# Layer 2's input product by seven half-size products for two of three pairs of chunks, and layer 2 in the order of the list scheduler

## Chip, cores and metric

One core of one Trainium2 chip. The metric is the device time of one execution in microseconds (us), the median of the runs. Engines: TensorE (PE; its weight loads PEld), VectorE (DVE), ScalarE (ACT), GpSimd (POOL), SyncE (SP, which issues most DMAs).

## What is computed

Attention with a threshold (4 batches, 8 heads, 576 positions, head size 64), then a gated layer with an RMS norm ("layer 1"), then a layer with a cosine ("layer 2"). The attention output is laid out as 2304 tokens by 512.

```python
# layer 1: x is 2304 x 512, w_gate and w_val 512 x 1536, w_out 1536 x 512
xn = x / sqrt(mean(x * x) + 1e-6) * rms_g
x = (silu(xn @ w_gate) * (xn @ w_val)) @ w_out
# layer 2: w_in 512 x 2048, w_out 2048 x 512
h = x @ w_in
out = (h * cos(h)) @ w_out
```

## The kernel before

**Matmuls.** Each operand of a product in the two layers is held as a rounded high part and a low rest (`hi`, `lo`, float32r), and `mm3` (L803 to L805) makes three matmuls of each 128-row step: high by high, high by rest, rest by high. All matmuls of both layers have line L805. A pair of weights arrives as 64-bit numbers; converting one 128x512 tile (`conv` in `moe`, L1032; `weight_job` for layer 2, L343) takes two bit operations on VectorE, a scaling on ScalarE and a sum on GpSimd; splitting it takes a copy on ScalarE and a subtraction on VectorE.

**Tokens** are worked on in 6 chunks of 384 (`TC`), as pairs (0,1), (2,3), (4,5).

**Attention and layer 1** are put in order by a list scheduler, `Plan`. Every step is added with its kind, a time at which it is due and what it needs, takes and frees (buffers counted by tag, as `c` for 4 PSUM banks of products, `h` for 6 hidden tiles, `w` for 6 weight tiles). `STEPS` gives each kind an engine, a duration in ns and an offset of its place in the order. `order()` simulates the engines and takes, again and again, the step that can start first, ties by place. Kinds in `LOCK` share one simulated port between VectorE and GpSimd; a GpSimd step in `BEHIND` also gets a wait for the last VectorE step that held the port.

**Layer 1's input products** (`block`, in `moe`) are made by seven products (`PROD`) where the plain form has eight: a block is a pair of chunks, and the gate and value tiles of one 128-column tile of the hidden layer. The seven use the weight combinations G, A22, S24, S31 and the token combinations B11, B21, B22, T1 to T4; VectorE adds the seven results up in SBUF tiles `r` (L1393), silu and product follow, then ScalarE's copy to `hi` (L1402) and GpSimd's subtraction for `lo` (L1406). Pairs (0,1) and (2,3) go together through the column tiles; (4,5) goes after them, with split weights that were stored to DRAM (`st`) and are loaded again (`re`).

**Layer 2** is not in the scheduler but in a loop written out by hand over 96 units: six groups of column tiles (`G2` = 3, 3, 3, 3, 2, 2 of 16), in each all six chunks in the order 2, 3, 0, 1, 4, 5. The unit's steps run shifted against each other: `in2` (12 matmuls into `ph`, 384 columns), `reduce2` (two ScalarE passes for the nearest number of turns), `reduce2_dve` (L1813 reads PSUM, L1814 only SBUF), `cos2` (|r| and sine on ScalarE, L1829, L1830), `mul2` (L1818, reads PSUM), `split2` (ScalarE's copy L1824, GpSimd's rest L1825), and five units later `o2` (9 matmuls of 512 columns into `po`). At the end of a group VectorE adds `po` to the sum in SBUF (L1865; the first group copies, L1863); after the last group the sum is stored. Weight conversions advance by `pump`, a step at a time between the units. `reduce2` to `mul2` work on the product as it lies in PSUM.

Of the kernel before, what the change touches and what calls it, by code (L numbers as in the profile page):

```python
# [21 lines left out]
C1 = 6.28125  # L22
C2 = 0.0019353071795864769
HALFPI = 1.5707963267948966

# [3 lines left out]
    "none": ("", 0, -4701467),  # L29
    "load_k": ("SP", 1700, -343212, 5000),  # L30
    "load_q": ("SP", 2300, -888717, 7000),
    "load_v": ("SP", 1700, 3657795, 5000),
    "pb": ("PE", 440, -612552),
    "pa": ("PE", 440, -4975920),
    "pc": ("PE", 355, 29040),
    "pb_a": ("ACT", 477, -6961829),
    "pa_a": ("ACT", 580, -3973655),
    "pc_a": ("ACT", 362, -1903561),
    "pa_l": ("DVE", 605, -5130676),
    "pb_l": ("DVE", 605, -4918818),  # L40
    "pc_l": ("DVE", 470, -6045594),
    "s": ("PE", 885, -6930363),
    "s4": ("PE", 790, 1242378),
    "warm": ("PE", 640, -112935),
    "max": ("DVE", 680, -10255673),
    "exp": ("ACT", 675, -1037703),
    "th": ("POOL", 300, -1060633),
    "mask": ("DVE", 742, -4138242),
    "t": ("PE", 445, 57622),
    "raw": ("ACT", 477, -6096088),  # L50
    "c0": ("PE", 245, -608604),
    "c1": ("PE", 465, -1489386),
    "c_raw": ("ACT", 295, -1524940),
    "radd": ("POOL", 250, -893656),
    "rinv": ("DVE", 375, 3655923),
    "r_out": ("SP", 2100, 2019715, 2500),
    "r_in": ("SP", 1700, -919170, 11000),
    "av0": ("PE", 2212, -4109991),
    "av1": ("PE", 2745, -1514959),
    "avo": ("ACT", 300, -7631444),  # L60
    "div": ("POOL", 1385, -204485),
    "xout": ("SP", 500, 2015089, 2500),
    "sq": ("POOL", 1122, 3600693),
    "x_add": ("POOL", 1385, 166922),
    "xsum": ("PE", 1085, 3874082),
    "mean": ("DVE", 140, -6653549),
    "rms": ("POOL", 1520, 56341),
    "rs_out": ("SP", 2500, -3692696, 2500),
    "x_load": ("SP", 500, 2189338, 6000),
    "x_p": ("POOL", 1010, 5504962),  # L70
    "x_a": ("ACT", 540, -4661274),
    "x_d": ("DVE", 480, -966896),
    "jdma": ("SP", 500, 3539250, 5000),
    "j1": ("DVE", 440, -3243245),
    "j2": ("DVE", 608, -11132166),
    "j_p": ("POOL", 1310, -67354),
    "j_a": ("ACT", 540, -7131505),
    "gv": ("PE", 2090, 5438925),
    "silu": ("ACT", 420, -6794675),
    "px": ("PE", 2090, -4699247),  # L80
    "pxc": ("ACT", 400, -137894),
    "hmul": ("DVE", 480, 75839),
    "hhi": ("ACT", 420, 1861687),
    "hlo": ("DVE", 480, 69979),
    "gv_": ("PE", 2090, -2378996),
    "silu_": ("ACT", 420, 78208),
    "px_": ("PE", 2090, -896324),
    "pxc_": ("ACT", 400, 615343),
    "hmul_": ("DVE", 480, 1858348),
    "hhi_": ("ACT", 420, -310574),  # L90
    "hlo_": ("DVE", 480, 1801274),
    "x_q": ("DVE", 480, -148421),
    "x_a_": ("ACT", 540, -603106),
    "x_d_": ("DVE", 480, -106794),
    "ld": ("SP", 500, 6072051, 4500),
    "st": ("SP", 500, 4800664, 3000),
    "re": ("SP", 500, 5444375, 3500),
    "wj1": ("DVE", 420, 17162),
    "wj2": ("DVE", 640, 22735),
    "wm": ("ACT", 650, 3870273),  # L100
    "wp": ("POOL", 1310, 4786433),
    "ws": ("POOL", 720, -5161440),
    "whi": ("ACT", 590, 3032813),
# [154 lines left out]
def attention_moe_cos_kernel(  # L258
# [127 lines left out]
    def pump(n_flying, **budget):  # L386

        for job in list(flying):
# [5 lines left out]
            if job[1] is None:  # L394
                flying.remove(job)
# [1524 lines left out]
```

## Time and profile before

| | us |
|---|---|
| three runs | 1126.11, 1126.55, 1128.15 (median 1126.55) |
| the profiled execution | 1124.69, with a span of 1122.7 from the first to the last instruction |
| attention, layer 1, layer 2 in the span | to about 290; about 337 to 709; 709 to the end |
| TensorE, VectorE, ScalarE, GpSimd busy | 1104.6, 927.3, 698.6, 412.7 |

The stages are cut where TensorE's first matmul of layer 2 stands (709.2), and where attention's matmuls have ended (about 290); between 290 and 337 layer 1's first units are made in the plain form. Matmuls overlap in the records: the time that one costs is read from a run of them in the chain of work that ended last, not from the duration of one.

### The profile page before, as it was taken

To read this page: it belongs to the slowest core of one execution; us is meant where nothing else is said; L and a number is where in the kernel's file an instruction comes from. 1 tells how busy PE (TensorE), PEld (TensorE's weight loads), DVE (VectorE), ACT (ScalarE), POOL (GpSimd) and SP (SyncE) were. 2 spreads that over 40 slices of the span, in tenths; PEclk is the share of its full clock that TensorE was granted. 3 is DMA by queue.
4 is the path that set the end of the run, shared out by engine and by line. 5 is a ranking of instruction groups with operands and counts; after the bars stand their busy time and mean duration, and the time that the engine had idled before them with its cause. 6 is when DMAs were issued, how large, how long until landed. Compare 5 with 4: busy or idle time off the path is not lost.

```text
span 1122.7 us, 19127 instructions
## 1 busy us (share of the span) xinstructions
PE 1104.6 (98%) x6868; PEld 998.8 (89%) x6868; DVE 927.3 (83%) x1773; ACT 698.6 (62%) x1312; POOL 412.7 (37%) x411
## 2 busy tenths in 40 slices
PE   8999999999999999999999999999999999999997
PEld 6777777777999999999999999899999999999995
DVE  6999999998799889788978757988787786877765
ACT  5888887887655534444434323777776776766663
POOL 1234246254423545655244412134333233332222
PEclk9999999999999999999999999999999999999999
DMA  6343352323425455632162754012111021100024
GB/s 129 96 113 104 99 147 73 89 83 92 144 97 186 169 188 198 248 133 65 39 197 91 253 202 148 1 57 57 57 57 57 1 73 41 39 19 1 1 58 112
DMA packets 113646, 112.61 MB, mean 100 GB/s; under 512 B 66672, under 2 KB 93072, under 8 KB 113552
## 3 DMA queue, kind: packets, MB, share of 16 engines
q1 hardware_dynamic: 112416, 111.10, 32.5%
q8 instruction: 54, 0.88, 0.3%
q10 hardware_dynamic: 1040, 0.26, 0.1%
q14 instruction: 40, 0.33, 0.1%
q0 software_dynamic: 96, 0.03, 0.0%
HBM read 82.97 MB, written 28.39 MB: 99 GB/s over the span
## 4 chain that ended last, share of the span: by engine, by line
PE 89%; DVE 5%; ACT 2%; DMA 2%; issue 1%; POOL 0%; SPq 0%; POOLq 0%; DVEq 0%; ACTq 0%
PE pc L805 21%; PE ph L805 17%; PE po L805 17%; PE px L805 13%; PE po L698 7%; PE s L571 6%; PE pst L661 5%; DVE e L621 1%; DVE s L592 1%; DMA raw<-in_moe_w_gate_dram 1%; PE psc L680 1%; ACT et L671 1%; DMA w<-wd 0%; PE psa L498 0%; DMA k<-in_k_dram 0%
## 5 line engine op out<-in xcount | busy, mean ns | idle before, releaser
L805 PE MATMUL ph<-xh,w 128*128 128x384 f32 x768 | 212.0, 337 | 0.0
L1825 POOL TENSOR_TENSOR hlo<-r,hhi 128x384 fp32r<-128x384 f32 x96 | 97.9, 1020 | 278.0 <-ACT hhi L1824 213.0
L805 PE MATMUL po<-w,hhi 128*128 128x512 f32 x576 | 180.4, 394 | 1.6 <-ACT hhi L1824 1.6
L1393 DVE TENSOR_TENSOR r<-r,pc 128x384 f32<-128x384 f32 x224 | 120.2, 551 | 45.6 <-PE pc L805 30.2
L805 PE MATMUL pc<-xh,w 128*128 128x384 f32 x512 | 146.2, 337 | 0.2 <-DVE hh L833 0.2
L805 PEld LDWEIGHTS ph<-xh,w 128*128 128x128 f32 x768 | 140.5, 188 | 3.9
L805 PE MATMUL ph<-xl,w 128*128 128x384 f32 x384 | 129.4, 337 | 0.0
L805 PEld LDWEIGHTS po<-w,hhi 128*128 128x128 f32 x576 | 107.0, 188 | 19.5 <-ACT hhi L1824 2.6
L805 PE MATMUL po<-w,hlo 128*128 128x512 f32 x288 | 114.2, 397 | 1.5 <-POOL hlo L1825 1.5
L1807 ACT ACTIVATE t<-ph,magic 128x384 f32<-128x384 f32 x96 | 55.7, 580 | 94.7 <-PE ph L805 94.4
L611 ACT ACTIVATE e<-s,m 128x576 f32<-128x576 f32 x128 | 96.6, 792 | 14.9 <-DVE s L592 14.7
L621 DVE SCALAR_TENSOR_TENSOR e<-s,th,e 128x576 f32<-128x576 f32 x128 | 104.7, 848 | 0.4 <-POOL th L602 0.4
L805 PE MATMUL px<-h,w 128*128 128x384 f32 x516 | 102.4, 338 | 0.3 <-DMA w<-wd 0.3
L1814 DVE SCALAR_TENSOR_TENSOR r<-t,r 128x384 f32<-128x384 f32 x96 | 97.0, 1010 | 3.3
L592 DVE TENSOR_SCALAR_CACHE_REDUCE s<-s 128x576 f32<-128x576 f32 x128 | 91.6, 752 | 5.9 <-PE s L571 5.5
L805 PEld LDWEIGHTS pc<-xh,w 128*128 128x128 f32 x512 | 94.1, 188 | 0.5 <-DVE hh L833 0.5
L805 PEld LDWEIGHTS px<-h,w 128*128 128x128 f32 x516 | 91.4, 188 | 0.6 <-PE pc L805 0.6
L1813 DVE SCALAR_TENSOR_TENSOR r<-t,ph 128x384 f32<-128x384 f32 x96 | 52.8, 550 | 45.3 <-ACT t L1808 45.0
L805 PE MATMUL pc<-xl,w 128*128 128x384 f32 x256 | 86.3, 337 | 0.0
L1054 POOL TENSOR_TENSOR wtmp<-wtmp,raw 128x512 int32<-128x512 int32 x42 | 54.6, 1314 | 81.4 <-DVE wtmp L1049 36.0
L671 ACT COPY et<-pst 128x512 f32<-128x512 f32 x144 | 78.0, 601 | 9.6 <-PE pst L661 9.1
L1865 DVE TENSOR_TENSOR acc<-acc,po 128x512 f32<-128x512 f32 x90 | 61.5, 687 | 22.9 <-PE po L805 22.0
(172 smaller groups left out, 2646.8 us busy)
## 6 DMA issues: line engine op xcount, KB each, us to landing
wd<-w SPq DMA_DIRECT2D x32, 512.0 KB
w<-wd SPq DMA_DIRECT2D x32, 512.0 KB
raw<-in_moe_w_out_dram SPq DMA_DIRECT2D x30, 512.0 KB
raw<-in_moe_w_in_dram SPq DMA_DIRECT2D x16, 512.0 KB
raw<-in_moe_w_gate_dram SPq DMA_DIRECT2D x14, 512.0 KB
raw<-in_moe_w_val_dram SPq DMA_DIRECT2D x14, 512.0 KB
x<-xb SPq DMA_DIRECT2D x16, 288.0 KB
kn<-in_k_dram SPq DMA_DIRECT2D x16, 256.0 KB
```

The costliest lines, as they stand in the source:

```text
L571: nc.tensor.matmul(un[n]["ps", hd][:, c, 0:288], lhs, kh[bb][r, k0:k0 + 288], start=i == 0, stop=i == 2,)
L592: nc.vector.tensor_scalar(s.rearrange("p (c n) -> p c n", c=2), un[n].pop(("ps", hd))[:, :, 0:288], qscale[:, 0:1] if n % 5 == 4 else 1.0, ...
L611: nc.scalar.activation(un[n]["e"][:, hd], un[n]["s", hd], AF.Exp, bias=grp[group_of(n)]["m"][:, c], scale=-1.0)
L621: nc.vector.scalar_tensor_tensor(e, un[n].pop(("s", hd)), grp[group_of(n)]["th"][:, ci:ci + 1], e, op0=ALU.is_le, op1=ALU.mult, accum_out= ...
L661: nc.tensor.transpose(ps[:, c], e[:, hd, k0:k0 + P], ident)
L671: nc.scalar.copy(dst, src)
L698: nc.tensor.matmul(po[64 * hd:64 * hd + 64, :], vn[:, c, hd, :] if c < 4 else vl[:, hd, :], hf[j]["et"][:, hd, c, :] if c < 4 else hf[j][" ...
L805: nc.tensor.matmul(ps, w[a], x[bb], start=first and i == 0, stop=last and i == 2)
L1393: vec.tensor_tensor(new(o) if fresh else tile_[o], src, ps[n], op=ADD)
L1814: nc.vector.scalar_tensor_tensor(r, t, -C2, r, op0=ALU.mult, op1=ALU.add)
L1825: nc.gpsimd.tensor_tensor(lo, r, f(hi), op=ALU.subtract)
L1865: nc.vector.tensor_tensor(dst, dst, oacc[c][t], op=ALU.add)
```

## The change

Layer 2 moves into `moe` and into the scheduler; the loop, `pump`, `need`, `split_job` and `weight_job`'s use for layer 2 go away. The input is scaled by 1/(2 pi) when it is split (`x2_halves`), so that the product comes out in turns.

Column tiles are taken in 8 pairs (`m`). First, for each m, the pair (2,3) in a block of seven products (`strassen2`) and the pair (0,1) plainly (`plain2`, 4 units of 12 matmuls); then the pair (4,5) in seven products for m = 7, 0, 1, ..., 6, with the split weights loaded again (`reload2`). The two column tiles of a pair take the place that gate and value have in layer 1. A block adds up its seven results in SBUF as layer 1 does. Then for each of four results comes `chain2`: the nearest whole turn (one ScalarE pass that adds a large number), the fraction (VectorE), |.| and sine (ScalarE), the product (VectorE), the high copy (ScalarE) and the rest (GpSimd). After a block, fraction and product have both operands in SBUF; in `plain2` they read PSUM as before. Output products (`out2`) are added up over one pair of column tiles: 6 groups of 6 matmuls of 512 columns a block, each then added to the sum in SBUF, 144 times in all where before it was 108, the first of them copies on ScalarE. Weights of layer 2 are split into G, A22, A21, S24, S31 with four GpSimd differences for each m (`weights2`).

Of the other edits: every place in `STEPS` is another number, those of attention and layer 1 too (the durations are the same); `tt` (6 buffers) becomes `tt` and `ttb` (3 each); the pools `r` and `a22` live to the end; chunks 0 and 1 get their tiles from the pools of 4 and 5.

```diff
-    "s": ("PE", 885, -6930363),
+    "s": ("PE", 885, -7406388),
...
+    "pr2": ("PE", 990, 4792230),
+    "oo": ("PE", 1390, 4798042),
+    "ra2": ("DVE", 550, -6470692),
+    "ct": ("ACT", 600, 3730880),
+    "cf": ("DVE", 550, 4442837),
+    "df": ("DVE", 530, -6637248),
+    "cb": ("ACT", 520, 3437175),
+    "cs": ("ACT", 620, 1491880),
+    "cg": ("DVE", 550, -3640286),
+    "dg": ("DVE", 530, -1697398),
+    "gh": ("ACT", 500, -5514388),
+    "gl": ("POOL", 1020, 4851894),
+    "oe": ("DVE", 690, 6452205),
...
+    "wj12", "wj22", "wp2", "ws2", "wlo2", "vlo2", "tz2", "tp2", "tlo2", "df", "dg", "gl",
 }
-BEHIND = {"div", "sq", "x_add", "x_p", "j_p", "wp", "ws", "tr", "rl"}
+BEHIND = {"div", "sq", "x_add", "x_p", "j_p", "wp", "ws", "tr", "rl", "wp2", "ws2", "gl"}
...
+        def x2_halves(c, k0, src, t, after):
+            def hi():
+                act.mul(x2t[c][0][:, k0:k0 + 2], src(), INV2PI)
+            def lo():
+                h, l = (q[:, k0:k0 + 2] for q in x2t[c])
+                vec.scalar_tensor_tensor(l, src(), INV2PI, f(h), op0=MUL, op1=SUB)
...
+            D, _ = split("a21", key("A21"), val(0, 2), t + 5, [e1, g5], [], False, "2")
+            s1 = add("ws2", at(t + 6), op(val(2, 4), val(0, 2), val(2, 4), ADD), after=[A])
+            s3 = add("ws2", at(t + 7), op(val(0, 2), gate(0, 2), val(0, 2), SUB), after=[s1, D, e0])
+            s2 = add("ws2", at(t + 8), op(gate(0, 2), val(2, 4), gate(0, 2), SUB), after=[s3, G])
+            s4 = add("ws2", at(t + 9), op(gate(2, 4), gate(2, 4), gate(0, 2), SUB), after=[s2])
+            S24, s24 = split("w", key("S24"), gate(0, 4), t + 10, [s4], [("tmp", ("2", m, 0))], save, "2")
+            S31, s31 = split("w", key("S31"), val(0, 4), t + 11, [s2], [("tmp", ("2", m, 1))], save, "2")
...
+            def turns():
+                act.activation(new("t2", "t", x), src(), AF.Identity, bias=magic[:, 0:1], scale=1.0)
+            def frac():
+                vec.scalar_tensor_tensor(g_tile[x], g_tile[x], MAGIC, src(), op0=SUB, op1=SUB)
+            def mul():
+                vec.scalar_tensor_tensor(g_tile[x], g_tile[x], TWOPI, src(), op0=MUL, op1=MUL)
...
+            y = add("ct", at(t - 60), turns, after=after, take=[("t2", ("t2", x))])
+            y = add("cf" if bank else "df", at(t - 60), frac, after=[y])
+            y = add("cb", at(t - 60), lambda: act.activation(g_tile[x], g_tile[x], AF.Abs), after=[y])
+            y = add("cs", at(t - 60), lambda: act.activation(
+                g_tile[x], g_tile[x], AF.Sin, bias=halfpi[:, 0:1], scale=-TWOPI), after=[y])
+            y = add("cg" if bank else "dg", at(t - 60), mul, after=[y], free=free)
+            y = hprev[0] = add("gh", at(t - 60), hi, after=[y, hprev[0]], take=[("h", ("h", x))])
+            hs2[x] = add("gl", at(t - 60), lo, after=[y], free=[("t2", x)])
...
+                    for kk in range(2):
+                        mm3(ps2[b, n], (w[0][:, a + kk], w[1][:, a + kk]), q[kk], kk == 0, kk == 1)
...
+        for m in range(NM):
+            weights2(m, t - 40)
+            strassen2(0, m, (2, 3), t)
+            plain2(m, (0, 1), t + SPAN_S)
+            t += SPAN_S + SPAN_P
+        lastplain = list(ends2[0, NM - 1, (0, 1)])
+        x_ready[4, 5] = x2_pair((4, 5), t - SPAN_P, last_out[4, 5], ends2[0, NM - 1, (2, 3)])
...
+        for m in (NM - 1,) + tuple(range(NM - 1)):
+            if m < NM - 1:
+                reload2(m, t - 25)
+            strassen2(1, m, (4, 5), t)
+            t += SPAN_S
```

## Rows read from the trace of the kernel before

**Rows 1.** Page, part 1: busy us, share of the span, instructions of each engine.
```profile
PE 1104.6 (98%) x6868; PEld 998.8 (89%) x6868; DVE 927.3 (83%) x1773; ACT 698.6 (62%) x1312; POOL 412.7 (37%) x411
```
**Rows 2.** Page, part 4: lines' shares of the chain that ended last.
```profile
PE pc L805 21%; PE ph L805 17%; PE po L805 17%; PE px L805 13%; PE po L698 7%; PE s L571 6%; PE pst L661 5%; DVE e L621 1%; DVE s L592 1%; DMA raw<-in_moe_w_gate_dram 1%; PE psc L680 1%; ACT et L671 1%; DMA w<-wd 0%; PE psa L498 0%; DMA k<-in_k_dram 0%
```
**Rows 3.** Windows: stretch, length, PE, PEld, DVE, ACT, POOL busy (instructions), clock, DMA.
```profile
0.00:290.00 290.00, 281.33 (x2469) 217.22 (x2470) 265.16 (x708) 231.52 (x423) 113.90 (x129) 1.00 0.41 103
...
337.00:709.20 372.20, 371.89 (x2119) 371.02 (x2118) 305.26 (x513) 154.70 (x294) 153.11 (x151) 1.00 0.47 159
709.20:1122.70 413.50, 404.54 (x2016) 364.04 (x2015) 314.37 (x487) 285.73 (x541) 132.14 (x122) 1.00 0.15 43
```
**Rows 4.** Chain that ended last from 700 us: start, us, what.
```profile
699.99 9.20 PE px L805 x53
709.18 4.24 PE ph L805 x24
...
728.37 2.11 PE ph L805 x12
...
738.85 2.09 PE po L805 x9
```
**Rows 5.** The same chain in layer 1.
```profile
503.17 3.16 PE pc L805 x18
```
**Rows 6.** Timeline, layer 2's first output product and last matmul: start, us, engine [idle before].
```profile
721.15 0.73 PE L805 MATMUL po<-w,hhi 128*128 128x512 f32 x2 [1.43 <-ACT hhi L1824]
...
1116.42 0.40 PE L805 MATMUL po<-w,hlo 128*128 128x512 f32 x1
```
**Rows 7.** Groups of layer 2, 709 to 1104 us: busy us, mean ns, idle before.
```profile
L1814 DVE SCALAR_TENSOR_TENSOR r<-t,r 128x384 f32<-128x384 f32 x95 | 96.4, 1015 | 3.3
L1825 POOL TENSOR_TENSOR hlo<-r,hhi 128x384 fp32r<-128x384 f32 x92 | 93.9, 1021 | 269.8 <-ACT hhi L1824 205.2 <-issue 64.6
...
L1865 DVE TENSOR_TENSOR acc<-acc,po 128x512 f32<-128x512 f32 x81 | 55.3, 686 | 17.5 <-PE po L805 16.7
...
L1813 DVE SCALAR_TENSOR_TENSOR r<-t,ph 128x384 f32<-128x384 f32 x95 | 52.3, 550 | 45.3 <-ACT t L1808 45.0
...
L365 DVE SCALAR_TENSOR_TENSOR wtmp<-raw,wtmp 128x512 int32<-128x512 int32 x26 | 17.8, 683 | 0.2
...
L378 DVE TENSOR_TENSOR w<-wtmp,w 128x512 fp32r<-128x512 f32 x26 | 17.4, 681 | 0.0
```
**Rows 8.** Line L1814 alone: ns least/median/most, first and last start.
```profile
L1814 DVE SCALAR_TENSOR_TENSOR r<-t,r x96: 557/1220/1349, 713.3 to 1107.3; 128x384 f32<-128x384 f32 x96
```
**Rows 9.** Groups of layer 1, 360 to 544 us, DVE and then POOL.
```profile
L1393 DVE TENSOR_TENSOR r<-r,pc 128x384 f32<-128x384 f32 x114 | 61.2, 550 | 19.4 <-PE pc L805 13.0 <-ACT r L1409 2.8 <-ACT r L1423 0.7
L1324 DVE TENSOR_TENSOR acc<-acc,px 128x768 f32<-128x768 f32 x30 | 28.5, 949 | 4.2 <-PE px L805 3.9
...
L1418 DVE TENSOR_TENSOR r<-r 128x384 f32<-128x384 f32 x16 | 11.7, 732 | 0.7
L1040 DVE TENSOR_SCALAR wtmp<-raw 128x512 int32<-128x512 int32 x24 | 10.0, 434 | 0.0
...
L1083 DVE TENSOR_TENSOR a<-wtmp,a 128x256 fp32r<-128x256 f32 x8 | 3.4, 431 | 0.0
...
L1054 POOL TENSOR_TENSOR wtmp<-wtmp,raw 128x512 int32<-128x512 int32 x24 | 31.1, 1314 | 33.2 <-DVE wtmp L1049 28.5 <-issue 4.6
L1124 POOL TENSOR_TENSOR wtmp<-wtmp 128x256 f32<-128x256 f32 x32 | 23.7, 741 | 10.2 <-DVE wtmp L1040 3.4 <-DVE r L1424 3.2 <-DVE a L1083 2.0
```
**Rows 10.** Windows, one pass of layer 1 with fresh weights.
```profile
360.00:406.00 46.00, 46.00 (x265) 46.00 (x264) 40.76 (x72) 19.33 (x36) 22.89 (x23) 1.00 0.49 171
```
**Rows 11.** Groups of ACT, the table load after attention.
```profile
L829 ACT ACT_TABLE_LOAD x1 | 1.3, 1283 | 0.0
```
**Rows 12.** Windows, layer 1 with reloaded weights; and PE's waits from 330 to 720 us.
```profile
640.00:660.00 20.00, 19.69 (x113) 19.40 (x112) 11.61 (x19) 6.29 (x12) 5.09 (x5) 1.00 0.74 264
...
PE px L805 <- DMA w<-wd: 0.3, 1, 0.3
```

## The prediction before the change was run

> **What bounds the kernel now.** I read the page's busy times first, then the windows by stage, then the chain of work that ended last, and only then single operations. TensorE is busy 1104.6 us, 98% of the span [rows 1], and the three dearest lines of the chain are all TensorE: layer 1's products pc 21%, layer 2's input product ph 17%, its output product po 17% [rows 2]. By stage [rows 3], attention (0 to 290 us) leaves TensorE 8.7 us idle, layer 1 (337 to 709) 0.3 us, layer 2 (709 to the end) 9.0 us, of which 5.9 lie after its last matmul. VectorE is busy 91%, 82% and 76% of these three stages. So both layers are bound by the number of matmuls, and a matmul that goes is time that goes, as long as the other engines keep pace. In the chain one ph step (12 matmuls of 384 columns) takes 2.11 us, 0.1758 us a matmul, and one po step (9 of 512 columns) 2.09 us, 0.2322 us [rows 4]. Layer 1's products, already made by seven, go at the same rate: 18 in 3.16 us, 0.1756 [rows 5].
>
> Layer 2 now is 96 units (6 chunks by 16 column tiles) of one ph and one po step: 96 x 4.20 = 403.2 us. It starts at 709.2 [rows 4] and its last matmul ends at 1116.8 [rows 6], 407.6 us later, so 4.4 us are stalls: the first output product waits 1.4 us in one piece for the first cosine [rows 6], the other 3 are smaller waits there and for the last cosines at the end.
>
> **The matmuls.** For a pair of chunks and a pair of column tiles the plain product is 2 x 2 x 4 x 3 = 48 matmuls; seven half-size products are 7 x 2 x 3 = 42. Output stays 6 x 6 = 36 matmuls. A seven-product block is 42 x 0.1758 + 36 x 0.2322 = 7.38 + 8.36 = 15.74 us, a plain block 8.44 + 8.36 = 16.80. There are 16 of the first (pairs (2,3) and (4,5), 8 pairs of column tiles) and 8 of the second: 251.8 + 134.4 = 386.2 us against 403.2. The change takes off 96 matmuls, 16.9 us.
>
> **VectorE.** While pair (2,3) and pair (0,1) go together, a double pass lasts 15.74 + 16.80 = 32.5 us on TensorE. VectorE has in it: 7 sums from PSUM at 0.550 [rows 9]; the plain chain's 4 fractions and 4 multiplications with one PSUM operand at 0.550 (as the row of L1813, rows 7); the block chain's 4 and 4 with both operands in SBUF, at 0.557 if undisturbed (least time of L1814, rows 8); 12 output sums at 0.687; four weight tiles' two bit steps at 0.434 and 0.683; five weight rests at 0.681 and two small ones at 0.431 [rows 7, 9]. That is 3.85 + 4.40 + 4.46 + 8.24 + 4.47 + 4.27 = 29.7 us, 91% of 32.5. Layer 1 is the yardstick: by the same durations a pass (28 sums, 8 wider output sums, 8 SBUF products, 6 weights) is about 40 us of 46, 88%, and there TensorE shows 46.00 of 46.00 busy with VectorE at 40.76 at most [rows 10]. So 91% is a little beyond what is shown to fit; I take no stall from it but 1 us in all, and keep up to 12 for the range. When pair (4,5) goes alone, a block has 3.85 + 4.46 + 4.12 = 12.4 us of VectorE in 15.7, with no weights to convert: covered.
>
> **GpSimd.** In the double pass: 8 rests at 1.02, 4 weight sums at 1.31, 4 differences at 0.74 = 16.4 us [rows 7, 9], half its time. But the operations do not run freely beside VectorE. L1813, which reads PSUM, has a mean of 0.550; L1814, the same operation with both inputs in SBUF, has 1.015, least 0.557, median 1.220 [rows 7, 8]: it meets the 1.02 us rest on GpSimd. Laid end to end, 16.4 us of GpSimd and the 13.2 us of VectorE with both operands in SBUF or on weights are 29.6 of 32.5. In layer 1, where a planner puts GpSimd's work behind VectorE's, the same kind of operation (L1418) has a mean of 0.732, not 1.015 [rows 9]. The new layer 2 is planned the same way; 8 x (0.732 - 0.557) = 1.4 us, 31.1 of 32.5: still under.
>
> The Trainium skill ("SBUF — State Buffer", section "Who interferes with whom") says that a VectorE instruction with two SBUF inputs and a GpSimd instruction that reads SBUF block each other for the whole instruction. The rows of L1813 and L1814 agree. It speaks against this change, since the block chain turns two PSUM operations of each cosine into SBUF ones; taken as a full loss at every meeting it is the third rival below.
>
> **ScalarE.** It is busy 285.7 of layer 2's 413.5 us, 69%, 0.53 us an instruction [rows 3]. A cosine now takes four passes in place of five, 96 x 0.5 = 51 us less; the new weight splits (24), first copies of products (16), operand splits and 36 first output copies, some 90 in all, are about 50 more: 70% still, covered. Silu and Sin now interleave at the seam, but the program loads a table at the first Silu and none for the later Sin [rows 11], so the seam costs no load.
>
> **DMA.** Splits are now stored and read again for pair (4,5): five tiles of 512 KB and one of 256, 2.9 MB in 15.7 us, 183 GB/s. Layer 1 does just this at up to 264 GB/s with one TensorE wait of 0.3 us [rows 12]. All go on SP's queue, where nothing but loads and final stores stands behind them. Cost 0, up to 3 if the cover of 25 us of lead is gone.
>
> **The seams.** At the start, the seven products need S24 and S31, and these wait for A21, whose buffer opens only after layer 1's last product: two small splits, three differences and a large split, about 0.8 + 3 x 0.74 + 1.3 + signals = 5 us. Behind it lie layer 1's last output products, now 9.2 us of TensorE alone [rows 4], and two products that need only G. Covered. The stall at 721 goes, because the first output product no longer follows two units behind. In the middle, pair (4,5)'s operands are split within the last plain block: some 8 wide VectorE operations of 0.95 [rows 9] and 4 narrow ones, together near 10, beside 8 of its own, in 16.8 us. A stall between 0 and 4; I take 1.5, since the first product needs just one operand. At the end, after the last product three cosine chains (0.55 + 4 x 0.53 + 2 x 0.557 + 1.02 = 4.8 us each, overlapping) stand before the last output products; some output of the block before may fill it. Of the 4.4 before, about 2 were there; I take 2, between 0 and 5. The closing (last sum, store) is 1122.7 - 1116.8 = 5.9 us and stays. Stalls in layer 2: 1 + 1.5 + 2 = 4.5, against 4.4 before.
>
> **Attention and layer 1.** Their operations stay, but nearly every step's place in the planner is new, so their order may move. Attention's 8.7 idle us are the most a better order could win; I take 0, with 4 each way.
>
> **Sum.** 386.2 + 4.5 + 5.9 = 396.6 against 413.5: -16.9. The profiled execution is 1124.69 us (span 1122.7); the median of the runs is 1126.55, 1.86 above. 1126.55 - 16.9 = 1109.7 us.
>
> **Rivals.**
> 1. *VectorE falls behind a little.* The SBUF operations of the block chain stretch to L1814's mean: 8 x 0.46 = 3.7 us more, 33.4 against 32.5, about 0.9 us in each of 7 double passes, 6 us, plus a middle seam at its bound (2.5): 1118. For it: VectorE at 91%, and weight work with no slack. Against it: layer 1 at 88% without a wait.
> 2. *The port decides, slower than before.* The operations stretch to L1814's median 1.220 and GpSimd loses as much: 29.7 + 5.3 = 35.0 in a double pass, 2.5 us x 7 = 17; in the blocks of pair (4,5) 12.4 + 4.1 (each of four rests meeting one operation) = 16.5 against 15.7, 0.8 x 8 = 6; 23 in all: 1133. It decides from a stretch of 2.8 us (the slack) + 17/7 = 5.2 us a double pass, a mean near 1.2 us for these eight operations; less only eats into the gain. Against it: layer 1's 0.732.
> 3. *The blocks do not run dense.* Four PSUM banks and six h tiles hold a block's results; a plain unit holds a bank through its whole chain. Were that over 4 x 4.2 = 16.8 us, TensorE would wait each time, and 0.7 us a block on 24 blocks would bring back 1126. Before, the first unit's way from its first matmul (709.2) to its finished cosine (721.15) is 12.0 us with an operation more [rows 4, 6], so I give it little.
> 4. *Better than forecast.* No stalls in layer 2 and 3 us won in attention: 1102.
>
> **How the numbers follow.** Forecast 0.64, rival 1 0.18, rival 2 0.10, rival 3 0.04, rival 4 0.04. The forecast's own range is 1104 to 1115 (attention 4 each way, seams 0 to 4). With most of rival 1 it becomes 1104 to 1120. A measurement of this kernel tells about 0.2%, 2.3 us, from no change. Faster by more: forecast, rivals 1 and 4, 0.86, of which I give 0.01 away to the unknown order of attention: 0.85. Within 0.2%: 0.05. Slower: 0.10.
>
> **What would show it.** TensorE's layer 2 should have 96 fewer 384-column matmuls at 0.176 us each; blocks of 15.7 and 16.8 us in the chain; TensorE busy over 99% between the seams; the SBUF operations of the chain near 0.6 to 0.75 us; VectorE near 90% in the first two thirds of layer 2 and under 80% in the last third. Waits of TensorE on VectorE's or GpSimd's results in mid-block would make rival 1 or 2 right; waits for a bank rival 3; another time of layer 2's start than 709 us would show that the order ahead of it moved.

## The result and the profile after

The changed kernel takes 1109.35 us, the median of four runs (1107.03 to 1110.96), against 1126.33 for the kernel before (four runs, 1125.27 to 1128.15): a ratio of 0.985, 95% interval 0.982 to 0.987. The profiled execution is 1108.63 us with a span of 1106.9, where before it was 1124.69 and 1122.7. All times below are of fast runs; one slow run, 2735.70 us of `e8_loads_later`, is left out.

The page's busy times after, by engine with their share of the span and the instructions, which answer to [rows 1]:

```profile
PE 1088.2 (98%) x6772; PEld 984.2 (89%) x6772; DVE 915.6 (83%) x1845; ACT 672.4 (61%) x1278; POOL 432.4 (39%) x443
```

TensorE has 96 instructions fewer and is busy 16.4 us less, at the same 98%. GpSimd and VectorE have more instructions, ScalarE fewer. The windows by stage after (stretch; busy time of PE, PEld, DVE, ACT, POOL with instructions; granted clock; DMA share; GB/s), cut where they were cut before, answer to [rows 3]. The line under "..." is the kernel before between 290 and 337 us, which [rows 3] leaves out:

```profile
0.00:290.00 290.00, 280.80 (x2464) 216.76 (x2465) 264.41 (x708) 231.13 (x422) 113.50 (x128) 1.00 0.40 101
290.00:337.00 47.00, 45.26 (x261) 44.64 (x260) 38.33 (x64) 24.66 (x51) 13.39 (x10) 1.00 0.37 123
337.00:709.20 372.20, 369.99 (x2099) 369.43 (x2098) 302.77 (x516) 157.36 (x303) 150.62 (x151) 1.00 0.47 160
709.20:1106.90 397.70, 392.12 (x1954) 353.36 (x1952) 310.11 (x560) 259.25 (x506) 154.86 (x154) 1.00 0.44 147
...
290.00:337.00 47.00, 46.84 (x270) 46.52 (x269) 42.54 (x67) 26.63 (x56) 13.51 (x10) 1.00 0.36 121
```

TensorE's idle time is 9.2 us in attention (8.7 before), 1.7 in the stretch after it (0.2), 2.2 in layer 1 (0.3) and 5.6 from 709.2 us on (9.0). So the new layer 2 gained more than the matmuls that went, and the stages ahead of it, whose operations did not change, lost something. TensorE's waits after, from 640 to 720 us (what it waited for: us in total, times, longest), show where two of these lie; from 720 us to its last matmul it has none:

```profile
PE px L815 <- DMA w<-wd: 2.2, 1, 2.2
PE pc L815 <- DVE w L1097: 0.7, 1, 0.7
```

Layer 2 begins in another place than before. TensorE's timeline after (start, length, line, operation; idle time before it and its releaser in brackets): the first product of layer 2, its one wait, and the last matmul of the kernel:

```profile
707.51 0.34 PE L815 MATMUL pc<-xh,w 128*128 128x384 f32 x1
...
710.86 0.62 PE L815 MATMUL pc<-th,w 128*128 128x384 f32 x2 [0.73 <-DVE w L1097]
...
1101.64 0.40 PE L815 MATMUL po<-wq,hlo 128*128 128x512 f32 x1
```

Layer 1's last 42 output products (px) now lie between layer 2's first blocks. The chain of work after (start, length, what), first these, then single steps of the dense part and its end, answers to [rows 4, 5]:

```profile
714.98 3.12 PE px L815 x18
...
722.28 2.08 PE px L815 x12
...
727.53 2.08 PE px L815 x12
...
771.91 6.99 PE po L815 x30
778.90 7.36 PE pc L815 x42
...
1102.08 0.69 DVE acc L1750
```

These 42 px take 3.12 + 2.08 + 2.08 = 7.3 us, 7.4 at 0.1758 each. Layer 2's own time is 1102.0 - 707.5 - 7.4 = 387.1 us, of which 0.7 is the one wait: 386.4 of work. One step of 42 pc takes 7.36 us, 0.1752 each, and 30 po take 6.99, 0.2330 each, as before the change. Counted without the 7.4 us, layer 1 would end at 707.5 + 7.4 = 714.9 us, where before it ended at 709.2: 5.7 later. So the span is accounted for: layer 2 from its first to its last matmul 387.1 against 407.6 (-20.5), the closing 4.9 against 5.9 (-1.0), all that lies ahead +5.7; together -15.8.

VectorE's groups after, from 705 us on (line, operation, tiles and shapes, count; busy time, mean ns; idle before and its releasers), against [rows 7, 8]:

```profile
L1626 DVE SCALAR_TENSOR_TENSOR t<-t,r 128x384 f32<-128x384 f32 x64 | 36.6, 572 | 3.1 <-ACT t L1639 2.9
L1623 DVE SCALAR_TENSOR_TENSOR t<-t,r 128x384 f32<-128x384 f32 x64 | 35.9, 567 | 3.0 <-ACT t L1620 2.7
```

The fraction (L1623) and the product (L1626) of a block's results have both operands in SBUF; they take 0.567 and 0.572 us, where the same kind of operation (L1814) took 1.015 before. And here is how busy the engines are in two stretches of the double passes and in one of pair (4,5) alone (windows after, columns as above):

```profile
780.00:860.00 80.00, 80.00 (x405) 72.85 (x404) 67.81 (x126) 56.86 (x113) 40.62 (x41) 1.00 0.43 146
860.00:940.00 80.00, 80.00 (x399) 71.98 (x398) 65.97 (x125) 54.72 (x107) 39.17 (x41) 1.00 0.48 167
1000.00:1080.00 80.00, 80.00 (x397) 71.99 (x396) 57.23 (x107) 45.86 (x89) 19.99 (x20) 1.00 0.42 136
```

TensorE is never idle; VectorE is at 84% in the first two and at 72% in the last. Its records overlap a little: the durations of VectorE's records (the mean of each group times its count) add up to 150.0 us from 780 to 940 us, over 250 instructions, and the window has 133.8 for the same 250; from 709.2 us to the end it is 342.4 against 310.1 for 560. Durations added up are 10 to 12% above the time that VectorE is taken.

### The profile page after: what moved, and what is told of

Its sections match the earlier page's. It is cut to its first block, busy times and chain, and to the rows that moved or that the text cites. A ratio compares the mean times of both kernels' runs of the same rounds, so it can differ in the third digit from the quotient of the medians.

```text
span 1106.9 us, 19279 instructions
## 1 busy us (share of the span) xinstructions
PE 1088.2 (98%) x6772; PEld 984.2 (89%) x6772; DVE 915.6 (83%) x1845; ACT 672.4 (61%) x1278; POOL 432.4 (39%) x443
## 4 chain that ended last, share of the span: by engine, by line
PE 91%; DVE 4%; DMA 2%; ACT 2%; issue 1%; POOL 1%; SPq 0%; DVEq 0%; POOLq 0%; ACTq 0%
PE pc L815 37%; PE po L815 18%; PE px L815 13%; PE po L708 7%; PE s L581 6%; PE pst L671 5%; PE pgv L815 1%; DVE e L631 1%; DVE s L602 1%; DMA x<-xb 1%; PE psc L690 1%; DMA w<-wd 1%; ACT et L681 1%; DMA k<-in_k_dram 0%; PE psa L508 0%
## 5 line engine op out<-in xcount | busy, mean ns | idle before, releaser
L815 PE MATMUL pc<-xh,w 128*128 128x384 f32 x896 | 255.9, 337 | 0.0
L815 PEld LDWEIGHTS pc<-xh,w 128*128 128x128 f32 x896 | 164.7, 188 | 2.5
L1408 DVE TENSOR_TENSOR r<-r,pc 128x384 f32<-128x384 f32 x224 | 120.5, 551 | 54.8 <-PE pc L815 42.5
L815 PE MATMUL pc<-xl,w 128*128 128x384 f32 x448 | 151.1, 337 | 0.0
L1634 POOL TENSOR_TENSOR h<-t,h 128x384 fp32r<-128x384 f32 x64 | 65.2, 1025 | 131.0 <-ACT h L1631 48.0
L1063 POOL TENSOR_TENSOR wtmp<-wtmp,raw 128x512 int32<-128x512 int32 x68 | 88.9, 1314 | 70.2 <-DVE t L1626 14.8
L815 PE MATMUL pc<-th,w 128*128 128x384 f32 x384 | 114.5, 339 | 0.7 <-DVE w L1097 0.7
L815 PE MATMUL po<-w,h 128*128 128x512 f32 x405 | 109.2, 394 | 0.0
L815 PEld LDWEIGHTS po<-w,h 128*128 128x128 f32 x405 | 75.5, 188 | 13.7
L815 PEld LDWEIGHTS pc<-xl,w 128*128 128x128 f32 x448 | 84.2, 188 | 2.5
L1678 DVE TENSOR_TENSOR r<-r,pc 128x384 f32<-128x384 f32 x112 | 60.5, 552 | 25.1 <-PE pc L815 22.8
L815 PEld LDWEIGHTS pc<-th,w 128*128 128x128 f32 x384 | 71.4, 189 | 2.0 <-DVE w L1097 1.0
```

The lines of the kernel that those rows point to most:

```text
L815: nc.tensor.matmul(ps, w[a], x[bb], start=first and i == 0, stop=last and i == 2)
L1063: pool.tensor_tensor(tmp[key], tmp[key], raw.pop(key)[:, :, :, 0], op=ADD)
L1408: vec.tensor_tensor(new(o) if fresh else tile_[o], src, ps[n], op=ADD)
L1634: pool.tensor_tensor(H[x][1], g_tile[x], f(H[x][0]), op=SUB)
L1678: vec.tensor_tensor(new("r", "r", (b, o)) if fresh else g_tile[b, o], s_, ps2[b, n], op=ADD)
```

## The experiments

All are made from the kernel after, unless said; L numbers are those of the kernel after. Times are medians; a ratio is to the kernel before in the same comparison, with its 95% interval.

### Is it the number of matmuls?

Pair (2,3) is made plainly again, with plain operands, and pair (4,5) stays in seven products:

```diff
...
-            strassen2(0, m, (2, 3), t)
+            plain2(m, (2, 3), t)
```

> The changed kernel with pair (2,3) of layer 2 made plainly too, in the scheduler: 8 blocks of seven products less, so 8 x 6 = 48 matmuls of 384 columns more. Theory 1 (layer 2 is bound by its matmuls, and the scheduler hides the rest): 48 x 0.1758 = 8.4 us slower than the changed kernel, about 1118, with no new wait of TensorE in layer 2. Theory 2 (the gain came from the scheduler's order, not from fewer products): same time as the changed kernel, within 2 us. Theory 3 (VectorE sets the pace of the double passes): no slower or faster, since a plain block has 3.9 us less of sums on VectorE.

Measured: 1113.88 us (1112.77 to 1114.52), ratio 0.990 (0.988 to 0.991). That is 4.5 us above after, so by its time none of the three theories is met: not 8.4 more, nor within 2 us, nor no slower. The trace shows what the 8.4 became. The first matmul of its layer 2 and its last:

```profile
704.52 0.34 PE L815 MATMUL pc<-xh,w 128*128 128x384 f32 x1
...
1105.75 0.40 PE L815 MATMUL po<-wq,hlo 128*128 128x512 f32 x1
```

Counted as above (42 px lie between them here too), its layer 2 takes 1106.15 - 704.5 - 7.4 = 394.2 us without a wait, against 386.4 of work in after: 7.8 us for 48 matmuls. But it starts 3.0 us earlier than in after and has no wait of 0.7, so its last matmul starts only 4.1 us later. Its waits from 640 us to the end and its windows at layer 1's end and in a double pass:

```profile
PE px L815 <- DMA w<-wd: 0.7, 2, 0.4
...
660.00:665.00 5.00, 4.57 (x27) 4.59 (x27) 2.60 (x5) 0.00 (x0) 0.00 (x0) 1.00 0.31 125
780.00:860.00 80.00, 80.00 (x404) 72.55 (x403) 57.41 (x102) 54.88 (x106) 38.92 (x40) 1.00 0.41 148
```

The wait for reloaded weights is 0.7 us in place of 2.2, and no slow stretch follows it (1.6 us in after, below). How much of this belongs to the edit is not shown: executions with the very order of after start layer 2 up to 2.8 us earlier than after's (below). In the double pass VectorE has 10 us in 80 less to do and TensorE gains nothing from it: inside layer 2 the change is worth its matmuls, and VectorE's load is no part of its price. A layer 2 that is all plain in the scheduler was not run, so what the scheduler gives by itself (by the traces 3.7 of layer 2's 20.5 us) is not separated by a run.

### How much slack has VectorE?

The sum of a seven-product block is made a second time, into a tile that nobody reads: first after all seven products, then after three of them (p6, p5, p3):

```diff
...
                     vec.tensor_tensor(new("r", "r", (b, o)) if fresh else g_tile[b, o], s_, ps2[b, n], op=ADD)
+                    vec.tensor_tensor(late["scr"], s_, ps2[b, n], op=ADD)
```

> The changed kernel, same order of steps, with each of the seven sums of a block of layer 2 made a second time on VectorE, into a tile that nobody reads: 7 x 0.55 = 3.85 us more of VectorE in each double pass and in each block of pair (4,5). Theory 1 (VectorE has the slack that its busy time in the windows shows: 133.8 of 160 us from 780 to 940, 27.2 of 32.5 us a double pass): 31.0 of 32.5, still covered, 0 to 4 us slower. Theory 2 (the slack is what the sum of the records' durations leaves, 29.7 of 32.5): 33.5 in 32.5, 1.0 x 7 = 7 us, and 16.3 in 15.7, 0.6 x 8 = 5 us: 12 us slower than the changed kernel, 1121.

> As the run with all seven sums doubled, but only three of a block's seven (after p6, p5 and p3): 1.65 us more of VectorE in each double pass and each block of pair (4,5). Both theories of the slack (27.2 or 29.7 of 32.5 us taken) leave it covered: 0 to 1 us slower than the changed kernel. If it costs more than 3 us, VectorE is nearer to its bound than either sum says.

Measured: seven more 1112.64 us (1109.09 to 1114.73), ratio 0.989 (0.986 to 0.991); three more 1108.72 (1106.41 to 1111.37), ratio 0.985 (0.983 to 0.988). With seven more, the windows of the double passes and TensorE's longest wait from 640 us on; with three more, one window:

```profile
780.00:860.00 80.00, 79.78 (x401) 71.94 (x401) 77.19 (x144) 55.51 (x110) 40.04 (x39) 1.00 0.41 139
860.00:940.00 80.00, 80.00 (x399) 71.90 (x398) 76.41 (x141) 56.14 (x111) 40.50 (x41) 1.00 0.51 177
...
PE px L815 <- DVE acc L1340: 2.1, 1, 2.1
```
```profile
780.00:860.00 80.00, 80.00 (x405) 72.85 (x405) 72.98 (x135) 57.43 (x113) 40.30 (x40) 1.00 0.42 144
```

At 96% VectorE still holds TensorE up for only 0.2 us in 160. With seven more the median is 3.3 us above after's, though the runs of the two overlap. The profiled execution (1109.09) is only 0.5 above, but its layer 2 takes 390.4 us in place of 387.1, counted as above, and what lies ahead of it, unchanged in order, happened to be 2.8 us shorter. 2.1 of the 3.3 us are one wait (px for L1340, at 721 us), where layer 1's last products meet layer 2's first doubled sums. So 112 more sums, 62 us of VectorE, cost about 3 us, as theory 1 has it and not theory 2 with its 12, and 0.2 of it in these double passes; three a block cost nothing that the runs tell. So the slack in a double pass is at least 3.9 us (seven sums of 0.55), and the reading by windows was right, that by added durations (29.7 + 3.9 = 33.6 of 32.5, an overflow) was not.

### Can a third pair follow?

Pair (0,1) goes by seven products too, with the operands of (2,3) in place of its own, so that only the time counts (the output rows of chunks 0 and 1 are of other tokens); the plain operand A21 is not made. A second kernel also has the weights of every pair of column tiles due 16 us earlier:

```diff
...
-            plain2(m, (0, 1), t + SPAN_S)
-            t += SPAN_S + SPAN_P
+            strassen2(0, m, (0, 1), t + SPAN_S)
+            t += 2 * SPAN_S
...
```
```diff
-            weights2(m, t - 40)
+            weights2(m, t - 56)
```

> The changed kernel with pair (0,1) of layer 2 in seven products too; it multiplies by the operands of pair (2,3) in place of its own, so the rows of chunks 0 and 1 of the output are those of other tokens, and A21 is not made. 48 matmuls less: -8.4 us if TensorE stays the bound (theory 1, about 1101). A double pass is then 31.5 us of TensorE and holds 2 x 8.3 + 8.2 + 8.3 = 33.1 us of VectorE by the sum of durations, 30.3 by the busy share of the windows (27.2/29.7). Theory 2 (sum of durations is the bound): 1.6 us x 7 = 11 us more, so 2 to 3 us slower than the changed kernel, about 1112, with TensorE waiting on VectorE in the double passes.

> The kernel with pair (0,1) in seven products too (by the operands of pair (2,3)), and all weight work of layer 2 due 16 us earlier (56 in place of 40 us ahead). The one without that took 1136 us with VectorE busy 82% in the double passes and TensorE waiting for weight splits. Theory 1 (the place of the weight work in the order makes the waits): most of them go, 10 us or more faster than 1136. Theory 2 (the buffers for weights and their intermediate tiles are full, so that earlier places change nothing): within 3 us of 1136.

Measured: 1136.17 us (1133.77 to 1136.88), ratio 1.009 (1.008 to 1.011); with the weights earlier 1137.33 (1132.83 to 1138.14), ratio 1.009 (1.007 to 1.011). 48 matmuls fewer and 27 us longer. The window of a double pass and TensorE's longest waits from 640 us on, of the first of the two:

```profile
780.00:860.00 80.00, 72.95 (x344) 64.26 (x345) 65.28 (x122) 49.84 (x97) 36.38 (x37) 0.96 0.41 145
...
PE pc L815 <- ACT w L1094: 6.7, 3, 3.7
PE po L815 <- DVE w L1097: 6.5, 2, 4.1
PE po L815 <- POOL h L1633: 3.9, 2, 3.3
```

Both expectations for the first kernel miss. VectorE is less busy than in after, so its throughput is not what decides; TensorE waits for split weights and for the rest of h, some 23 us in all in its layer 2, and after the waits its clock falls (0.96 in the window).

The second kernel tells nothing more. A due time enters a step's place with 1000 a us, so 16 us are 16,000, while the offsets of the kinds in `STEPS` lie up to millions apart; here the steps come out in the same order on every engine. It is the first kernel a second time, with the same three waits within 0.2 us (6.9, 6.5 and 3.9), and that its time meets its theory 2 shows nothing of buffers. Nor would an earlier due time help by itself: in the traces of after and of the first kernel each of the 26 weight loads issued after 700 us starts 0.03 us behind a sum on GpSimd (L1063) that frees one of the two `raw` tiles. But after has this too and does not wait. The edit also keeps S24 and S31 in their `w` tiles through the second block, where after frees them behind the first. Which of these, or what else, sets off the waits was not tried and stays open.

### Is it the planned order that keeps VectorE and GpSimd apart?

The kinds of layer 2 are taken out of the shared port and of the waits behind VectorE:

```diff
-    "wj12", "wj22", "wp2", "ws2", "wlo2", "vlo2", "tz2", "tp2", "tlo2", "df", "dg", "gl",
 }
-BEHIND = {"div", "sq", "x_add", "x_p", "j_p", "wp", "ws", "tr", "rl", "wp2", "ws2", "gl"}
+BEHIND = {"div", "sq", "x_add", "x_p", "j_p", "wp", "ws", "tr", "rl"}
```

> The changed kernel with none of layer 2's steps in the scheduler's shared port (LOCK) and with GpSimd's steps of layer 2 no longer told to wait for VectorE's (BEHIND). Theory 1 (the planned port is why VectorE's fraction and product in SBUF stay at 0.57 us): their mean rises to the 1.0 to 1.2 us that L1814 has before, VectorE gets 8 x 0.5 = 4 us more a double pass, 31 to 34 of 32.5 us, and the kernel 2 to 12 us slower. Theory 2 (they meet GpSimd seldom anyway): mean under 0.7 us, no slower.

Measured: 1111.58 us (1109.99 to 1112.99), ratio 0.987 (0.985 to 0.988). VectorE's two SBUF operations from 730 to 965 us, in this kernel (one line number less) and then in after:

```profile
L1625 DVE SCALAR_TENSOR_TENSOR t<-t,r 128x384 f32<-128x384 f32 x28 | 20.3, 725 | 2.6 <-ACT t L1638 2.6
L1622 DVE SCALAR_TENSOR_TENSOR t<-t,r 128x384 f32<-128x384 f32 x28 | 19.5, 703 | 0.0
```
```profile
L1623 DVE SCALAR_TENSOR_TENSOR t<-t,r 128x384 f32<-128x384 f32 x28 | 16.1, 584 | 1.2 <-ACT t L1620 1.1
L1626 DVE SCALAR_TENSOR_TENSOR t<-t,r 128x384 f32<-128x384 f32 x28 | 15.6, 561 | 0.6 <-ACT t L1639 0.5
```

The plan does keep them apart. Of layer 2's 128 operations of this kind, 7 overlap one of GpSimd in the trace of after and 35 here; the 35 take 0.89 us on average, the other 93 take 0.55. (Before, 65 of the 96 of L1814 overlap one and take 1.23; the other 31 take 0.56.) So the mean rises by 0.14 us in this stretch, to 0.71 and not to the 1.0 of the kernel before: theory 1 has the cause right and its size wrong. TensorE loses nothing in the double passes (80.00 of 80 in both stretches from 780 to 940 us). The median is 2.2 us above after's, with runs that overlap; TensorE's waits in layer 2, 4.1 us in all, lie before 736 us, and one of them (1.2 us) is for a product of VectorE (L1625). The Trainium skill ("SBUF — State Buffer", section "Who interferes with whom") has a VectorE instruction with two SBUF inputs contend with a GpSimd instruction that reads SBUF, and calls the shared port an exclusive lock. The direction agrees; but 11 of the 35 are no longer than an undisturbed one.

### Do the new places cost anything ahead of layer 2?

Four kernels. In the first, the kinds that both kernels have get the places of before:

```diff
-    "load_k": ("SP", 1700, 3411947, 5000),
+    "load_k": ("SP", 1700, -343212, 5000),
...
```

> The changed kernel with the places that the kernel before gives to the kinds of steps of attention and layer 1 (the kinds of layer 2 keep theirs). In the changed kernel layer 1 ends some 5.7 us later than before: 1.7 us of new waits between attention and layer 1 (290 to 337 us), a wait of 2.2 us for a weight reload near 662 us with some 1.6 us of half clock behind it, 0.5 us at the start. Theory 1 (the new places did it): both waits go, layer 2 starts about 4 us earlier, 1104 to 1106 us. Theory 2 (the loads of layer 2's weights in the same queue did it, whatever the places): the wait between attention and layer 1 goes (-1.7 us), the reload wait stays or grows, 1107 to 1111.

In the second, the kernel before gets the places of after for the same kinds:

> The kernel before with the places that the changed kernel gives to the same kinds; layer 2 stays the written-out loop. Theory 1 (the new places cost attention and layer 1 their time by themselves): 2 to 5 us slower than before, 1128 to 1132. Theory 2 (they cost nothing without the changed layer 2 behind them): within 1.5 us of before.

In the third, only attention's kinds and those of the plain units that follow it (`load_k` to `x_d_` in `STEPS`) get their old places; in the fourth, the first weights of layer 2 are also due later (the edit of the next experiment):

> The changed kernel with the places of before for the kinds of attention and of layer 1's first units only (load_k to x_d_); weights, blocks and layer 2 keep the new places. Theory 1 (the waits of 1.7 us between attention and layer 1 come from these kinds' places): they go and nothing is lost behind, 1.5 to 2 us faster than the changed kernel, about 1107.5. Theory 2 (what is won there is lost again in layer 1, as with all old places): within 1 us of the changed kernel.

> Old places for the kinds of attention and layer 1's first units, and layer 2's first weight work due 12 us later, both in the changed kernel. If both waits were separate and nothing took their place, 5 us faster than the changed kernel, about 1104; if the later loads gain nothing, as their times alone say, the same as with the old attention places alone.

Measured: all old places 1110.04 us (1109.61 to 1111.5), ratio 0.986 (0.984 to 0.987); the kernel before with the new places 1131.12 (1130.77 to 1137.05), ratio 1.005 (1.003 to 1.008); attention's old places 1122.20 (1119.29 to 1123.82), ratio 0.997 (0.995 to 0.998); the fourth 1120.88 (1118.08 to 1122.01), ratio 0.995 (0.994 to 0.996). The later due time changes no step's order (see the next experiment), so the fourth is the third kernel a second time.

With all old places, the windows of the stretch after attention and of layer 2's start, and TensorE's waits from 640 us on:

```profile
290.00:337.00 47.00, 46.95 (x271) 46.63 (x270) 41.84 (x65) 25.34 (x52) 14.04 (x10) 1.00 0.36 122
709.00:780.00 71.00, 67.32 (x346) 61.44 (x345) 55.82 (x99) 51.98 (x103) 37.04 (x36) 1.00 0.44 156
...
PE px L815 <- DMA w<-wd: 2.0, 2, 1.8
PE pc L815 <- DVE t L1626: 1.8, 1, 1.8
PE pc L815 <- ACT w L1094: 1.7, 1, 1.7
```

As theory 2 has it, the 1.7 us after attention are won back and the wait for reloaded weights stays; and TensorE is idle for 3.7 us at layer 2's start, where in after it is for 0.7. With the old places in both, the kernel before (1126.54 in that comparison) and the changed one are 16.5 us apart, so the gain does not come from the places.

The kernel before, with the new places, is as its theory 1 has it: some 5 us slower by the medians, without any of the rest of the change. Its profiled execution is its longest (1137.05); there TensorE is idle for 1.6 us in the stretch after attention (45.36 busy of 47, clock 0.93; before 0.2), and its wait for reloaded weights has grown from 0.3 us:

```profile
PE px L805 <- DMA w<-wd: 1.6, 2, 1.5
```

And with only attention's old places, TensorE waits 4.9 us in one piece in layer 1 (px for hlo L850) and 3.1 for reloaded weights. So the places of the stages hang together: no set of them taken over alone kept what it won. Both expectations for the third kernel miss; taking half the old places is far worse than taking all or none.

### Why do the reloaded weights come late?

The weights of layer 2's first pair of column tiles are made due 12 us later, which was to put their loads behind layer 1's reloads:

```diff
-            weights2(m, t - 40)
+            weights2(m, t - (40 if m else 28))
```

> The changed kernel with the weight work of layer 2's first pair of column tiles due 12 us later (28 in place of 40 us ahead of its use), so that its loads and conversions stand behind layer 1's reloads near 650 us. Theory 1 (those two loads of 512 KB in SP's queue and on the DMA engines delay the reload that TensorE waits for): the wait of 2.2 us and the half clock after it go, 3 to 4 us faster than the changed kernel, 1105 to 1107. Theory 2 (the reload is late by itself, as the 0.3 us wait before the change hints): the wait stays, within 1 us. If S24 comes too late, a wait of TensorE at layer 2's start (0.7 us now) grows.

> The kernel with the weight work of layer 2's first pair of column tiles due 12 us later, again, for its profile. By its first times (about 1110) the later loads gain nothing. Theory 1 (the loads delay layer 1's reload): TensorE's wait for the reload near 662 us is under 0.5 us, and what it gains (2.2 us and the half clock) is lost at layer 2's start, where S24 and S31 come later: waits there of 2 us or more. Theory 2 (the reload is late by itself): the wait near 662 us is still 1.5 to 2.5 us and layer 2's start as in the changed kernel.

Measured: 1110.15 us (three runs, 1108.35 to 1110.69), ratio 0.985 (0.984 to 0.987); made again, 1108.70 (1106.65 to 1109.67), ratio 0.985 (0.983 to 0.986). The edit changes nothing: as with the third pair, the due time is too small a part of a step's place, and the steps come out in the order of after on every engine. So neither theory is tested. But the trace is that of a second execution of after's program, and the two differ. TensorE's wait for reloaded weights from 640 to 720 us and two windows of this execution:

```profile
PE px L815 <- DMA w<-wd: 2.2, 2, 1.8
...
660.00:665.00 5.00, 3.43 (x20) 3.46 (x21) 1.47 (x4) 0.00 (x0) 0.00 (x0) 1.00 0.55 219
665.00:670.00 5.00, 5.00 (x30) 5.00 (x29) 4.14 (x6) 1.55 (x3) 1.01 (x1) 1.00 0.49 133
```

and the same two windows of after's own trace, a third inside them, and its timeline:

```profile
660.00:665.00 5.00, 2.79 (x12) 2.50 (x11) 0.55 (x1) 0.00 (x0) 0.00 (x0) 0.82 0.73 292
665.00:670.00 5.00, 5.00 (x26) 5.00 (x26) 3.25 (x6) 0.14 (x1) 0.00 (x0) 0.84 0.06 9
664.00:666.00 2.00, 2.00 (x8) 2.00 (x7) 0.00 (x0) 0.00 (x0) 0.00 (x0) 0.50 0.05 18
...
662.58 1.75 PE L815 MATMUL px<-h,w 128*128 128x384 f32 x6 [2.21 <-DMA w<-wd]
664.13 0.52 PE L815 MATMUL pc<-th,w 128*128 128x384 f32 x1
664.45 0.52 PE L815 MATMUL pc<-tl,w 128*128 128x384 f32 x1
...
667.36 0.34 PE L815 MATMUL pc<-th,a 128*128 128x384 f32 x1
```

After the wait of 2.21 us the granted clock is 0.50 from 664 to 666 us, matmuls follow each other by 0.32 us there (384 columns at the lower of the two levels, 1.2 GHz), and 18 of them take from 662.58 to 667.36, 4.8 us in place of 3.2. The other execution waits 1.8 and then 0.5 us and keeps its full clock. The two kernels with doubled sums have after's order too, as far as layer 2. With seven more the wait is 1.4 us and the clock stays full; with three more the wait is 2.2 us and the clock falls again:

```profile
660.00:665.00 5.00, 2.79 (x11) 2.82 (x11) 0.55 (x1) 0.00 (x0) 0.00 (x0) 0.77 0.70 279
```

So the length of this wait, and the slow stretch behind it, change from one execution of this order to the next. Counted as above, layer 1 would end at 714.9 and 715.2 us in the two with the slow stretch and at 712.9 and 712.1 in the two without, against 709.2 before.

Why the weights are late stays open. In after, two loads of layer 2's `w_in` (512 KB each) stand in SP's queue between layer 1's reloads (647.19 to 652.05 us), and the DMA was busy 0.73 from 660 to 665 us, at 292 GB/s. But the kernel before with the new places, which lacks the new layer 2, waits 1.5 us as well, and the changed kernel with the old places 1.8. Neither alone accounts for the wait, and no run separates them.

No version here is measurably faster than the kernel after: 1108.70 is its own program again, and 1108.72 (three more sums) lies within its runs.

## Why the prediction was right, and where it was not

**The matmuls** (-16.9 us predicted, -16.8 read). 386.2 us of work was the sum and 386.4 is read, at 0.175 and 0.233 us a matmul; undoing half the change cost 7.8 of 8.4 us within layer 2. This was the step that carried the result. (The 403.2 us before are counted, not read: by [rows 3] the old layer 2 was idle for 9.0 - 5.9 = 3.1 us up to its last matmul and not for the 4.4 of the prediction, so some 1.3 us of what is called stalls was work.)

**VectorE** (1 us of stall predicted, none found in the double passes). The sum was a little short: 29.7 us of 32.5 a double pass were predicted, and the durations in the trace add up to 150.0 of 160, 30.5 of 32.5. But the window's busy time is 133.8 of 160, 27.2 of 32.5, 84% and not 91%, because records overlap. The yardstick was short by more: the forecast put layer 1 at "about 40 us of 46", 88%, by the same durations, but in the kernel before they add up to 171.0 us of 184 from 360 to 544, 93% (155.9 by the window), with TensorE never idle. So 91% was not "a little beyond what is shown to fit" but less than what fitted already, and both the stall of 1 us and much of rival 1's chance came from that count. With seven sums more, durations add up to 173.5 us in 160, more than there is, and TensorE idles 0.2 us.

**GpSimd and the port** (0.73 us an operation taken, 0.57 found; 0.71 without the plan). Rival 2, which one sentence of the prediction calls the third, needed means near 1.2 us. Neither its cause nor its price is seen in after, and even with the plan's protection gone TensorE showed no wait for it from 780 to 940 us.

**ScalarE** (70% predicted). 259.3 of 397.7 us, 65%: covered as said, with 18 first output copies where the sum had 36.

**The seams** (3.5 us predicted, 0.7 found). Start: taken at 0, found 0.7, as a wait of TensorE for one split weight (L1097); layer 1's last products do cover the rest. The middle (1.5 taken): TensorE has no wait there at all. The end (2 taken): the last po run on without a gap, since output of the block before fills the last cosine's time, as the text allowed. Mis-sized by 2.8 us, with the lower ends (0 and 0) the right ones; with VectorE's 1 us that makes 3.8.

**The closing** (5.9 predicted, 4.9 found): taken as unchanged, it is 1 us shorter. One output sum of 0.69 us stands behind the last product in both kernels; behind it SP issues stores for another 1.1 us in after and 2.3 before, where the last three sums came in a row.

**Attention and layer 1** (0 predicted, bounds 4 each way; +5.7 found in the profiled execution). This step failed. The 5.7 us are 0.5 in attention, 1.6 in the stretch from 290 to 337 (1.3 of it the wait of L748 for L739), 1.9 more of waiting for reloaded weights, and 1.6 of half clock behind that wait: 5.6. Three other executions of the same order have +6.0, +3.7 and +2.9, so about 3 us came with the change each time and the rest with the execution; two of the four lie beyond the bounds. The new places alone cost the kernel before some 5 us (e2_before_new_places). "I take 0" was argued from attention's idle time, which could only be won; that a stage without idle time can only lose was not counted. And the DMA step priced only layer 2's own reloads, which were never waited for; layer 1's reloads, where the old wait was 0.3 us [rows 12], were not looked at, and that wait with its half clock is 3.5 of the 5.7 us.

**The sum.** Ahead of layer 2 +5.7, seams and VectorE's stall -3.8, closing -1.0, work +0.2 against the forecast: +1.1 us in the profiled span, -15.8 in place of -16.9. The medians came out at -17.0. So the time was met to 0.35 us because two misses of opposite sign nearly cancelled, and that closely by luck besides: three sets of runs of this one program have medians of 1109.35, 1110.15 and 1108.70. Of the rivals none came true. TensorE waited in mid-block only when a third pair was added, and whether that was rival 3's cause is not shown.

## What to carry to other kernels

Where TensorE shows no waits, count the matmuls: 96 fewer at 0.1758 us are 16.9, and 16.8 were read. Measure an engine's slack by its busy share in windows, and by doubling one of its operations, not by adding up the durations of its records. A list scheduler with new places moves the stages that nobody changed: price their seams on both sides, and add to a wait what the clock may lose after it. Before reading an experiment on due times, compare the order of steps: three of the edits here changed none. And profile one program more than once before a wait of 2 us is put down to a change.

## What the runs showed of the hardware that was not expected

One order of work, executed four times, waited 1.4 to 2.2 us at one place; behind the two longer waits TensorE ran at the lower clock level (0.50 from 664 to 666 us in after, 1.6 us lost), behind the two shorter ones (1.4 and 1.8) at the full one. But the wait's length does not decide alone: the third and the fourth kernel of the places are one program, both profiled executions waited 3.1 us for reloaded weights, and the windows behind the wait (third, then fourth) are these:

```profile
675.00:680.00 5.00, 5.00 (x17) 5.00 (x17) 1.02 (x2) 0.00 (x0) 0.00 (x0) 0.50 0.07 28
675.00:680.00 5.00, 5.00 (x31) 5.00 (x30) 3.46 (x6) 0.34 (x1) 0.00 (x0) 1.00 0.14 21
```

VectorE ran at 96% busy in a stretch of 80 us (77.19) with TensorE idle for 0.2 us of it, and its records overlap by some 9% of their durations in layer 2 (342.4 us added up, 310.1 by the window, a ratio of 0.91).
